# A chunked linear-attention kernel with a maxout feed-forward: units of two sequences, transposed attention output, and both layers side by side

## The chip, the cores and the metric

The kernel runs on one core of one Trainium2 chip. The metric is device time in microseconds (us), the median over repeated executions. A ratio below is the mean time of a kernel's fast runs over the mean time of the kernel before in the same rounds on the same chip, so it is not quite the ratio of the quoted medians. The engines are PE (matrix), DVE (vector), ACT (scalar, activation functions), POOL (general purpose) and SP, which only issues transfers here.

## The reference

```python
# attention: 4 sequences, 8 heads, 768 steps, head width 48
for t in range(S):
    cur = einsum('bhd,bhe->bhde', u[None] * k_t, v_t)
    y[:, :, t] = einsum('bhd,bhde->bhe', r_t, state + cur)
    state = w_t[:, :, :, None] * state + einsum('bhd,bhe->bhde', k_t, v_t)
# feed-forward on x = y as (3072 tokens, 384)
g = maximum(x @ w1, x @ w2)      # (384, 1024) each
out = g @ w_out                  # (1024, 384)
```

Both kernels use max(a, b) = (a + b + |a - b|)/2. The sum goes straight through a combined matrix wc = (w1 + w2) w_out, and only |x (w1 - w2)| has to be formed. The factor 1/2 is applied to the output in the kernel before, and to w_out once, at the start, in the changed one (the "scaling of w_out" below).

## The kernel before

A chunk is 128 steps of one sequence; there are 24. The decay products are the exponential of a running sum of ln w, which a matmul with a triangle makes. Each chunk loads its inputs, forms the decayed r and k, transposes them, builds a masked 128x128 product per head, multiplies it with v, adds the state's part, and updates the state. All attention comes first; the feed-forward follows from a buffer x_sb.

```python
            nc.scalar.activation(lw, wt, AF.Ln)                       # table load
            nc.tensor.matmul(excl_p, triU, lw...)                     # running sum
            nc.scalar.activation(Aexcl..., excl_p, AF.Exp)            # table load
            # ... (cut)
            for h in range(H):                                        # 16 a chunk
                nc.tensor.matmul(Wtot_p[:, h:h + 1], lw[:, h, :], ones_col)
            # ... (cut: transposes, masked product MTm)
            for h in range(H):
                nc.tensor.matmul(y_p[:, h * D:(h + 1) * D], MTm[:, h, :], vb[:, h, :],
                                 start=True, stop=(c == 0))           # 128 rows
                if c > 0:
                    nc.tensor.matmul(y_p[:, h * D:(h + 1) * D], rT[:, h, :],
                                     S_b[:, h, :], start=False, stop=True)   # 48 rows
            # ... (cut: y into x_sb, state update on DVE)
    # after all chunks:
        for fo in range(FO):
            g1 = mps.tile([C, MBN], F32, tag="g1")                    # one buffer
            # ... (cut: three matmuls into g1)
            nc.scalar.activation(gT[:, fo, :], g1, AF.Abs)
```

## Time and profile before

| | before |
|---|---|
| time | 424.39 us at first, 424.6 beside the changed kernel |
| head, attention, feed-forward | 46, 256, 120 us |
| PE, DVE, ACT busy in attention | 203, 189, 93 of 256 us |
| granted PE clock in attention | 0.51 |
| one chunk of one sequence, steady | 10.88 us |

The prediction below shows the windows, the timeline and the groups. Two more views matter. The first is the page's row of 40 equal slices of the span, in tenths; PEclk is the granted clock of PE.

```profile
PE   1158899887788887788887788875788778787872
DVE  1872667777877777777777877885122222232212
PEclk9998565555555555555555555555799999999997
```

Three quarters busy on both PE and DVE, at half the clock, and then a feed-forward with DVE mostly idle: after the seventh slice none has an engine at 90%. The second is one group (count, then busy us and mean ns, then idle time of the engine ahead of it and who ended it):

```profile
L210 PE MATMUL g<-xT,wd_sb 128*128 128x512 bf16 x138 | 41.4, 391 | 13.5 <-ACT gT L212 12.4
```

In the feed-forward PE waits 12.4 us for ACT, since g has one buffer.

### The profile page before, as it was taken

Reading aid. Unit: us, or ns where it says so; the run is one execution under the profiler, and the core shown is the slowest. Engines: PE = TensorE matmul, PEld = TensorE weight load, DVE = VectorE, ACT = ScalarE, POOL = GpSimd, SP = SyncE. Lnnn points to the kernel's source line nnn. Section 1 sums busy time; section 2 is a strip of 40 time slices with the busy share of each in tenths; the row PEclk is TensorE's granted clock in tenths of the full one; section 3 lists DMA queues with packets and bytes.
Section 4 is the critical chain, followed back from the end, with each engine's and each line's share of the span. In section 5 each row is a group of like instructions: output and inputs, shape, how many; then the busy total and the mean of one; then the engine's idle time right before and its main releaser. Section 6 shows DMA issues by size and latency. Waiting matters only on the chain.

```text
span 422.0 us, 5555 instructions
## 1 busy us (share of the span) xinstructions
PE 314.5 (75%) x2078; PEld 189.2 (45%) x2088; DVE 244.0 (58%) x596; ACT 142.7 (34%) x206; POOL 2.7 (1%) x16
## 2 busy tenths in 40 slices
PE   1158899887788887788887788875788778787872
PEld 0125666555455554555555455542333334343331
DVE  1872667777877777777777877885122222232212
ACT  1014652444444443443333532100233243323320
POOL 2000000000000000000000000000000000000000
PEclk9998565555555555555555555555799999999997
DMA  7995242442433333433344222000001111110111
GB/s 293 186 251 91 53 80 56 76 74 57 82 75 66 70 68 57 89 67 72 74 75 76 56 57 57 2 0 0 2 25 50 33 44 37 39 50 29 54 43 51
DMA packets 112076, 28.67 MB, mean 68 GB/s; under 512 B 101041, under 2 KB 111282, under 8 KB 112050
## 3 DMA queue, kind: packets, MB, share of 16 engines
q1 hardware_dynamic: 112050, 28.32, 32.5%
q8 instruction: 16, 0.26, 0.3%
q14 instruction: 10, 0.08, 0.1%
HBM read 23.59 MB, written 4.72 MB: 67 GB/s over the span
## 4 chain that ended last, share of the span: by engine, by line
PE 53%; DVE 18%; ACT 17%; DMA 6%; issue 5%; SPq 0%; ACTq 0%; DVEq 0%
PE g L210 9%; PE Wtot_p L141 7%; PE y_p L168 6%; ACT gT L212 6%; PE y_p L171 6%; PE op L216 5%; ACT L116 5%; PE tp_k L154 5%; DVE MTm L164 4%; PE mt_p L163 3%; DVE x_sb L175 3%; PE op L219 3%; PE tp_r L153 3%; DVE S_new L184 2%; DMA w2f<-in_moe_w_dram 2%
## 5 line engine op out<-in xcount | busy, mean ns | idle before, releaser
L118 PE MATMUL excl_p<-lw,triU 128*128 128x384 f32 x48 | 38.8, 910 | 34.2 <-DVE incl L122 33.5
L143 ACT ACTIVATE Wtot_b<-Wtot_p 48x384 f32<-48x384 f32 x24 | 11.6, 484 | 120.8 <-DVE S_new L184 119.6
L210 PE MATMUL g<-xT,wd_sb 128*128 128x512 bf16 x138 | 41.4, 391 | 13.5 <-ACT gT L212 12.4
L205 DVE COPY xT<-tp 128x128 bf16<-128x128 bf16 x72 | 16.1, 224 | 54.0 <-PE tp L204 54.0
L212 ACT ACTIVATE gT<-g 128x512 bf16<-128x512 f32 x48 | 28.7, 597 | 53.5 <-PE g L210 52.7
L216 PE MATMUL op<-gT,wo_sb 128*128 128x512 bf16 x140 | 41.6, 381 | 3.8 <-ACT gT L212 2.5
L227 DVE CAST osx<-tp 128x128 f32<-128x128 bf16 x72 | 20.8, 289 | 40.7 <-PE tp L225 27.6
L168 PE MATMUL y_p<-vb,MTm 128*128 128x48 bf16 x192 | 38.1, 220 | 5.7 <-DVE MTm L164 5.7
L141 PE MATMUL Wtot_p<-ones_col,lw 128*48 128x1 f32 x384 | 33.2, 216 | 5.2 <-ACT lw L116 3.5
L141 PEld LDWEIGHTS Wtot_p<-ones_col,lw 128*48 128x48 f32 x384 | 31.2, 186 | 10.5 <-ACT lw L116 7.8
L171 PE MATMUL y_p<-S_b_new,rT 48*128 48x48 bf16 x160 | 34.8, 218 | 0.0
L156 DVE COPY kT<-tp_k 48x512 bf16<-48x512 bf16 x48 | 19.9, 414 | 23.2 <-PE tp_k L154 23.1
L164 DVE TENSOR_TENSOR MTm<-mt_p,maskU 128x512 bf16<-128x512 f32 x48 | 31.0, 686 | 2.7 <-PE mt_p L163 0.2
L153 PE MATMUL tp_r<-ident,rp 128*48 128x128 bf16 x192 | 29.8, 308 | 2.8 <-DVE rp L127 2.5
L153 PEld LDWEIGHTS <-rp 128*48 128x48 bf16 x192 | 18.3, 145 | 26.9 <-DVE vb L131 16.2
L154 PE MATMUL tp_k<-ident,kp 128*48 128x128 bf16 x192 | 29.8, 309 | 0.7 <-DVE kT L156 0.4
L163 PE MATMUL mt_p<-rT,kT 48*128 48x128 bf16 x192 | 28.3, 302 | 0.5 <-DVE kT L156 0.5
L116 ACT ACT_TABLE_LOAD x22 | 28.2, 1283 | 1.1 <-PEq L248 0.7
L118 PEld LDWEIGHTS excl_p<-lw,triU 128*128 128x128 f32 x48 | 11.8, 305 | 37.0 <-DVE incl L122 35.8
L120 ACT ACT_TABLE_LOAD x22 | 28.2, 1283 | 0.4
L210 PEld LDWEIGHTS <-wd_sb 128*128 128x128 bf16 x144 | 13.9, 98 | 31.7 <-issue 22.8
L168 PEld LDWEIGHTS <-MTm 128*128 128x128 bf16 x192 | 18.4, 106 | 19.3 <-DVE MTm L164 12.5
(56 smaller groups left out, 408.2 us busy)
## 6 DMA issues: line engine op xcount, KB each, us to landing
rt<-in_r_dram SPq DMA_DIRECT2D x24, 192.0 KB, 3.8
kt<-in_k_dram SPq DMA_DIRECT2D x24, 192.0 KB, 3.6
vt<-in_v_dram SPq DMA_DIRECT2D x24, 192.0 KB, 2.7
wt<-in_w_dram SPq DMA_DIRECT2D x24, 192.0 KB, 3.1
out_dram<-osx SPq DMA_DIRECT2D x72, 64.0 KB, 1.5
w1f<-in_moe_w_dram SPq DMA_DIRECT2D x1, 1536.0 KB, 6.4
w2f<-in_moe_w_dram SPq DMA_DIRECT2D x1, 1536.0 KB, 9.9
wof<-in_moe_w_out_dram SPq DMA_DIRECT2D x1, 1536.0 KB, 7.1
```

The lines of the kernel that those rows point to most:

```text
L116: nc.scalar.activation(lw, wt, AF.Ln)
L118: nc.tensor.matmul(excl_p, triU, lw.rearrange("a b c -> a (b c)"))
L141: nc.tensor.matmul(Wtot_p[:, h:h + 1], lw[:, h, :], ones_col)
L153: nc.tensor.transpose(tp_r[:, j, :], rp[:, h, :], ident)
L154: nc.tensor.transpose(tp_k[:, j, :], kp[:, h, :], ident)
L163: nc.tensor.matmul(mt_p[:, j, :], kT[:, h, :], rT[:, h, :])
L164: nc.vector.tensor_mul(MTm[:, half * 4:half * 4 + 4, :], mt_p, maskU4)
L168: nc.tensor.matmul(y_p[:, h * D:(h + 1) * D], MTm[:, h, :], vb[:, h, :], start=True, stop=(c == 0))
L171: nc.tensor.matmul(y_p[:, h * D:(h + 1) * D], rT[:, h, :], S_b[:, h, :], start=False, stop=True)
L210: nc.tensor.matmul(g1, wd_sb[:, ko, fo * C:(fo + 1) * C], xT[:, ko, :], start=(ko == 0), stop=(ko == KO - 1))
L212: nc.scalar.activation(gT[:, fo, :], g1, AF.Abs)
L216: nc.tensor.matmul(op, wo_sb[:, fo, ko * C:(ko + 1) * C], gT[:, fo, :], start=(fo == 0), stop=False)
```

## The change

The intent is to let attention and feed-forward run on the engines at the same time, with fewer and longer instructions and a single load of ACT's tables. A unit is one chunk of two sequences (12 units). The output of attention is made already transposed, in slices of 128 columns, so the feed-forward needs no transposes. Because a head has 48 columns and a slice has 128, v and the state are kept in zero-padded rows (vz, S_z), and a matmul takes a 128-wide window of such a row. The feed-forward of unit i-1 is written after the attention of unit i. The diff, cut to its core:

```diff
+    units = [(c, bp) for c in range(NC) for bp in range(B // NB)]
+    nc.scalar.preload_act_table_set("natural_log_exp_and_others")
 # ... inputs: one tile of [C, 2 sequences, H, D] each instead of [C, H, D]
-            Wtot_p = psum.tile([D, H], F32, tag="wt")
-            for h in range(H):
-                nc.tensor.matmul(Wtot_p[:, h:h + 1], lw[:, h, :], ones_col)
+            row = dram.tile([1, NB * HD], F32)      # last row of incl out to DRAM
+            nc.sync.dma_start(out=row, in_=incl[C - 1:C]...)
+            for ab in range(2):                     # and back, transposed
+                nc.sync.dma_start(out=Wt[ab * DP:ab * DP + D]..., in_=row...[ab])
+            nc.scalar.activation(Wx, Wt, AF.Exp)
-            vb = sbuf.tile([C, H, D], BF16, tag="vb")
-            nc.vector.tensor_copy(vb, vt)
+        nc.gpsimd.tensor_copy(vz[...], t["v"])      # POOL
 # ... transposes: two heads (padded to 64 rows each) in one
-                nc.tensor.matmul(y_p[:, h * D:(h + 1) * D], MTm[:, h, :], vb[:, h, :], ...)
-                if c > 0:
-                    nc.tensor.matmul(y_p[:, h * D:(h + 1) * D], rT[:, h, :], S_b[:, h, :], ...)
+            for j in range(KO):
+                nc.tensor.matmul(y_p[:, j, :], vd[:, b, j * C:(j + 1) * C], ident, ...)
+            if c > 0:
+                for p, j, o in s_win:
+                    nc.tensor.matmul(y_p[:, j, :], S_z[bp][:, b, p * SS + o:p * SS + o + C],
+                                     rkT[:, 0, p, :], ...)
+            for n, (h, j, o) in enumerate(v_win):
+                nc.tensor.matmul(y_p[:, j, :], vz[:, b, h * VS + o:h * VS + o + C],
+                                 MTm[:, h % 2, h // 2, :], ...)
+            nc.scalar.copy(xT[:, :, b, :], y_p)
 # ... state update on DVE, its bf16 copies on POOL
+    t = load(0); load_w12(); t_next = load(1); load_wo()
+    for i in range(len(units)):
+        xT = attention(i, t)
+        if i == 0:
+            prep_weights()
+        if prev is not None:
+            feed_forward(i - 1, prev)       # g in two buffers, output not transposed
+        prev = xT
+        # ... load(i + 2)
```

## The prediction

Passages on the hardware that no trace of the kernel before showed are cut from the text below, and each cut is marked. One cut is a term of the forecast's sum: an allowance for DVE held up by POOL, which took the walk's period from 14.0 to 14.8 us. The sum still has it: 42 + 10 x 14.8 + 15 + 2.4 = 207.4 us.

> **What bounds the kernel now.** I read four views: the windows table, the timeline of one steady chunk, the groups, and the chain of waits in the last stage. The windows first (busy us and count of each engine, then granted clock, DMA share, GB/s):
>
> ```profile
> 0.00:46.00 46.00, 20.39 (x140) 12.98 (x140) 23.70 (x37) 12.17 (x17) 2.66 (x16) 0.92 0.93 193
> 46.00:302.00 256.00, 203.20 (x1489) 134.86 (x1490) 188.73 (x431) 92.81 (x127) 0.00 (x0) 0.51 0.31 59
> 302.00:422.00 120.00, 90.92 (x450) 41.34 (x458) 31.56 (x128) 37.67 (x64) 0.00 (x0) 0.98 0.14 40
> ```
>
> There are three stages one after the other: a head of 46 us that waits for transfers, an attention stage of 256 us, and a feed-forward of 120 us. In attention PE is 79% busy but at a granted clock of 0.51; in the feed-forward it runs at 0.98, and DVE is idle for three quarters of it. Neither stage uses what the other leaves free.
>
> The timeline shows a chunk repeating every 10.9 us (the table load of L116 starts at 143.37 and 154.24). What fills PE in it is not arithmetic:
>
> ```profile
> 157.80 0.53 PE L180 MATMUL kv_p<-vb,kp 128*48 128x48 bf16 x8
> ...
> 160.51 0.22 PE L168 MATMUL y_p<-vb,MTm 128*128 128x48 bf16 x1 [0.21 <-DVE MTm L164]
> 160.66 0.22 PE L171 MATMUL y_p<-S_b_new,rT 48*128 48x48 bf16 x1
> 160.81 0.22 PE L168 MATMUL y_p<-vb,MTm 128*128 128x48 bf16 x1
> ```
>
> Eight alike kv_p matmuls of 48 columns take 0.53 us, so (0.53 - 0.22)/7 = 0.045 us each. The y_p matmuls of the same 48 columns, which alternate between 128 and 48 rows of the array, start 0.15 us apart: 0.1 us is lost at each change of form, 16 times a chunk.
>
> ```profile
> L118 PE MATMUL excl_p<-lw,triU 128*128 128x384 f32 x48 | 38.8, 910 | 34.2 <-DVE incl L122 33.5
> L141 PE MATMUL Wtot_p<-ones_col,lw 128*48 128x1 f32 x384 | 33.2, 216 | 5.2 <-ACT lw L116 3.5
> L164 DVE TENSOR_TENSOR MTm<-mt_p,maskU 128x512 bf16<-128x512 f32 x48 | 31.0, 686 | 2.7 <-PE mt_p L163 0.2
> L116 ACT ACT_TABLE_LOAD x22 | 28.2, 1283 | 1.1 <-PEq L248 0.7
> L120 ACT ACT_TABLE_LOAD x22 | 28.2, 1283 | 0.4
> ```
>
> The 44 table loads cost ACT 56 us, and in every chunk one of them and the Wtot_p matmuls behind it are on the chain. In the feed-forward the chain is a handshake, because one buffer holds g:
>
> ```profile
> 303.60 0.82 PE g L210 x3
> 304.44 0.61 ACT gT L212
> 305.09 0.82 PE g L210 x3
> 305.93 0.61 ACT gT L212
> ```
>
> Each fo costs 1.49 us of which PE streams 0.65.
>
> [...]
>
> **The change part by part.** A unit is one chunk of two sequences, and there are 12. I count each engine's work per unit at durations of this trace.
>
> DVE. In a run of instructions the starts are closer than the durations: three of 384 elements start at 153.86, 154.33 and 154.80, so 0.47 us each; the 3072-element subtraction takes 3.36 against 0.545 us, so 1.05 ns an element and 0.07 us fixed. That gives 0.87 us for 768 and 1.14 us for 1024 elements. Per unit: incl 2 x 0.47; rp, kp, ku twice, the reduce and vd 6 x 0.87 = 5.2; the masked product 2 x 1.14; the state 3 x 0.47; the rkT copies 2 x 0.62 (the 128x1024 bf16 copy from PSUM took 0.69 with its fixed part). The sum is 11.1 us, against about 8 a chunk, or 16 for two, before. Gone are the casts of v and S, the add into x_sb, both transposing copies of the feed-forward, and half of the fixed costs.
>
> PE at full clock. A 512-column matmul streams in 0.215 us (three take 0.81, one 0.38), 0.42 ns a column. The feed-forward is 24 x 256 + 22 x 384 columns = 6.1 us. Attention has 16 transposes, 16 mt_p and 38 y_p matmuls of 128 columns, at an estimated 0.065 us (half of the 0.105 measured at half clock, plus something; two 128-column ones started 0.06 apart in the feed-forward): 4.5 us. ex_p in fp32 2 x 0.7, kv_p 0.5, six changes of form 0.6. The sum is 13.2 us; the arithmetic grows (padded windows), but the 384 Wtot_p matmuls and the alternation go. At half clock it would be about 25 us.
>
> ACT: Ln and Ainv 0.8 each, Aex 2 x 0.42, four gT 2.1, xT and osb 1.7, Wx 0.2: 6.4 us, no table loads. POOL: the v copy and two state copies, perhaps 2 us. Input transfers: four loads of 192 KB were issued one a microsecond while the queue was full (12.10 to 16.3), so 8.4 us a unit: hidden, if the period exceeds it.
>
> Clock. Matmuls other than transposes stream about 9 us of a 14 us unit. In the feed-forward before, it is 12 of 20 us, at clock 0.98. So I take full clock.
>
> Order. I walked one unit through the orders in which the engines' instructions are built. From MTm of sequence 1: PE does the rest of o_p and the y windows, then ex_p of the next unit at about 4.3 us, and DVE waits some 0.9 us for it; Aex, incl, rp; kp waits about 0.7 us for Ainv, which stands behind a gT on ACT; g_p is paced by ACT until about 8; then the k transposes, rkT at 9.4, MTm of sequence 0 at 11, mt_p of sequence 1 done at 13.9. So the period is about 14.0, set by turns by PE and DVE.[...]
>
> Head. Unit 0 loads first (1.57 MB, 8.3 us), then w1 and w2 (3.1 MB, about 9.5 us as before), unit 1 (8.3 us), w_out (about 5 us): w_out lands near 34 us, where it landed at 25.4. DVE's scaling of w_out stands ahead of unit 1's rkT, and the 24 wc_p matmuls (5.5 us[...]) stand ahead of its mt_p. So MTm of unit 1 starts at about 42 us. Ten periods later unit 11 is there; its rest (3 us), y, g_p, o_p of the last feed-forward and its store take about 15 us. Time = 42 + 10 x 14.8 + 15 + 2.4 (time less span before) = 207.4; I say 208.
>
> **The rivals.**
> - The clock stays low:[...] attention before ran at 0.50 while 79% busy. Then PE binds at 25 us: 42 + 250 + 18 = 310 us. Against it: the feed-forward matmuls lie throughout the unit[...]. 5%; a partly low clock (period 18, 240 us) another 10%.
> - A new wait: the row of incl goes to DRAM and comes back through the same queue as the loads in 4-byte pieces, and Wx waits for it on ACT ahead of xT. I place its landing near 11.5 us after the unit's start and its use at 14. If each of the transfers takes 2 us longer, it stands on the path: period 17, 230 us.
> [...]
> - Everything overlaps better than in my walk and PE alone binds: period 13.2, 191 us.
> - The gain of the overlap fails and only fixed costs are saved: attention 200 and feed-forward 90, about 340. Nothing in the order supports it.
>
> **Range and chances.** One microsecond of the period is 10 us of the time. A period of 13 to 17.5 with the same head and tail gives 189 to 234; I take 188 to 240. Even the worst rival named stays 20% below 424, so faster is nearly sure: 0.98, with 0.01 each for the rest.
>
> **What would show it right or wrong.** Right: no ACT_TABLE_LOAD but the first; clock above 0.9 from 60 us on; a spacing of 14 to 15.5 us between the ex_p pairs; DVE near 75% and PE near 85% busy in the steady part; the first MTm of unit 1 at 40 to 44 us; waits of DVE for ex_p and Ainv of under 1 us a unit. Wrong: a clock near 0.5 (first rival); ACT's longest wait being Wx for its transfer (second);[...] a steady period outside 13 to 17.5; or a head beyond 50 us.

## The result, and the profile after

The changed kernel took 192.44 us (192.05 to 193.31, four runs) beside 424.6 us (424.07 to 424.91, four runs); the ratio is 0.4537, with a 95% interval of 0.4525 to 0.4549. The profiled run took 193.31 us at a mean clock of 0.998.

The slices of the kernel after (rows as before) show one busy stage behind a head:

```profile
PE   0615875389999989999999999999999999999992
DVE  0169998975747988999899799798997997937300
PEclk9999999999999999999999999999999999999999
```

Two windows, the end of the head and one steady unit (busy us and count of PE, weight loads, DVE, ACT and POOL, then granted clock, DMA share, GB/s):

```profile
30.00:40.00 10.00, 5.30 (x38) 2.80 (x38) 9.29 (x12) 2.07 (x3) 0.00 (x0) 1.00 1.00 189
...
108.65:121.30 12.65, 12.36 (x138) 8.69 (x137) 11.34 (x16) 6.67 (x13) 2.43 (x3) 1.00 0.77 154
```

One unit takes 12.65 us in the steady part. It holds two chunks of attention and the feed-forward of 256 tokens. PE is busy for 12.36 us of it and DVE for 11.34. Before, two chunks took 21.8 us and the feed-forward of 256 tokens a further 10 us (120/12).

The handshake is nearly gone (groups view): PE's idle time ahead of g fell from 13.5 to 1.1 us.

```profile
L262 PE MATMUL g_p<-xT,wd_sb 128*128 128x256 bf16 x288 | 39.8, 272 | 1.1
```

The timeline of one steady unit shows what is packed how densely:

```profile
105.88 1.30 PE L272 MATMUL o_p<-wo_sb,gT 128*128 128x384 bf16 x7
107.02 0.81 PE L158 MATMUL ex_p<-lw,triU 128*128 128x384 f32 x2
...
108.39 0.56 DVE L160 TENSOR_TENSOR incl<-ex_p,lw 128x384 f32<-128x384 f32 x1 [0.95 <-ACT Aex L159]
...
112.59 0.40 PE L209 MATMUL mt_p<-rkT 48*128 48x128 bf16 x8
114.89 0.72 PE L225 MATMUL y_p<-MTm,vz 128*128 128x128 bf16 x10 [0.20 <-DVE MTm L210]
```

With about 0.22 us for a lone matmul (the median of L225 is 219 ns), ten y_p matmuls in 0.72 us are (0.72 - 0.22)/9 = 0.056 us apart. The eight mt_p matmuls, which read 48 rows from row 0 and 48 from row 64 by turns, are (0.40 - 0.22)/7 = 0.026 us apart. Busy time takes in the tail of each burst and pauses shorter than it, so it is not all work. At the measured spacings (0.109 us for g_p, 0.163 for o_p, 0.325 for ex_p, 0.0125 for kv_p) the matmuls of a unit add up to 11.1 us of its 12.65. PE and DVE (11.34) thus have about the same amount of work, and neither alone fills the unit. DVE's only long wait is 0.95 us: its ex_p stands in PE's order behind seven o_p matmuls, and Aex (0.49 us on ACT) comes before incl.

The head is the rest of the story. Its timeline, just before unit 1 gets going:

```profile
37.17 1.75 DVE L111 TENSOR_SCALAR wo_sb<-wof 128x3072 bf16<-128x3072 f32 x1
...
38.98 6.57 PE L120 MATMUL wc_p<-wo_sb,wsT_sb 128*128 128x384 bf16 x24 [1.48 <-DVE wo_sb L111]
45.48 0.40 PE L209 MATMUL mt_p<-rkT 48*128 48x128 bf16 x8
...
45.92 1.23 DVE L210 TENSOR_TENSOR MTm<-mt_p,triU 128x1024 bf16<-128x1024 f32 x1 [2.11 <-PE mt_p L209]
```

The 24 wc_p matmuls take 6.57 us, but not evenly: the first 16 start 0.32 us apart, the last eight 0.163, as the same 384 columns do in the steady part (seven in 1.30, less 0.33 for one, over six: 0.162). So PE ran at half rate until about 44 us, though the record of its clock shows full speed there (1.00 from 30 to 40 and from 40 to 60 us); read PEclk and the mean clock of this profile with that in mind. The first masked product of a unit (MTm) starts at 45.92 for unit 1, 63.50 for unit 2, and 175.60 for unit 11. So the profiled time is 45.9 (head) + 129.7 (ten units) + 15.9 (tail) + 1.8 (time less span).

### The profile page after: what moved, and what is told of

It is laid out like the page before. It is cut to its first block, busy times and chain, and to the rows that moved or that the text cites. A ratio compares the mean times of both kernels' runs of the same rounds, so it can differ in the third digit from the quotient of the medians.

```text
span 191.5 us, 3963 instructions
## 1 busy us (share of the span) xinstructions
PE 163.8 (86%) x1624; PEld 111.7 (58%) x1624; DVE 145.3 (76%) x184; ACT 83.3 (43%) x158; POOL 41.3 (22%) x52
## 4 chain that ended last, share of the span: by engine, by line
PE 48%; DVE 25%; issue 8%; ACT 8%; DMA 5%; SPq 3%; POOL 1%; ACTq 0%; DVEq 0%; POOLq 0%
PE o_p L272 13%; PE g_p L262 8%; PE y_p L225 7%; DVE MTm L210 6%; PE ex_p L158 5%; DVE sf L241 5%; DVE ku L186 4%; PE o_p L269 4%; ACT gT L265 4%; PE wc_p L120 3%; DMA u_b<-in_u_dram 3%; ACT Ainv L163 3%; SPq L130 3%; PE y_p L217 3%; PE mt_p L209 3%
## 5 line engine op out<-in xcount | busy, mean ns | idle before, releaser
L262 PE MATMUL g_p<-xT,wd_sb 128*128 128x256 bf16 x288 | 39.8, 272 | 1.1
L272 PE MATMUL o_p<-wo_sb,gT 128*128 128x384 bf16 x192 | 40.0, 327 | 0.0
L265 ACT ACTIVATE gT<-g_p 128x512 bf16<-128x512 f32 x48 | 27.9, 596 | 12.0 <-PE g_p L262 11.7
L210 DVE TENSOR_TENSOR MTm<-mt_p,triU 128x1024 bf16<-128x1024 f32 x24 | 29.3, 1221 | 3.5 <-PE mt_p L209 3.2
L158 PE MATMUL ex_p<-lw,triU 128*128 128x384 f32 x48 | 23.1, 567 | 7.9 <-ACT lw L153 6.7
L160 DVE TENSOR_TENSOR incl<-ex_p,lw 128x384 f32<-128x384 f32 x24 | 13.3, 554 | 21.3 <-ACT Aex L159 21.3
L272 PEld LDWEIGHTS <-gT 128*128 128x128 bf16 x192 | 17.8, 98 | 10.0
L166 POOL CAST vz<-vt 128x768 bf16<-128x768 f32 x12 | 11.1, 928 | 47.0 <-DMA vt<-in_v_dram 38.2
L225 PEld LDWEIGHTS <-vz 128*128 128x128 bf16 x240 | 16.2, 102 | 6.5 <-issue 4.5
L225 PE MATMUL y_p<-MTm,vz 128*128 128x128 bf16 x240 | 18.4, 226 | 1.7 <-DVE MTm L210 1.7
L269 PE MATMUL o_p<-wc_sb,xT 128*128 128x384 bf16 x72 | 17.3, 326 | 0.0
L203 DVE COPY rkT<-tp 128x1024 bf16<-128x1024 bf16 x24 | 16.4, 683 | 0.5 <-PE tp L200 0.5
```

The lines of the kernel that those rows point to most:

```text
L158: nc.tensor.matmul(ex_p, triU, lw[:, b].rearrange("p h d -> p (h d)"))
L160: nc.vector.tensor_add(incl[:, b].rearrange("p h d -> p (h d)"), ex_p, lw[:, b].rearrange("p h d -> p (h d)"))
L203: nc.vector.tensor_copy(rkT, tp)
L210: nc.vector.tensor_mul(MTm.rearrange("p a q c -> p (a q) c"), mt_p.rearrange("p a q c -> p (a q) c"), triU.unsqueeze(1).to_broadcast([C, H ...
L225: nc.tensor.matmul(y_p[:, j, :], vz[:, b, h * VS + o:h * VS + o + C], MTm[:, h % 2, h // 2, :], start=False, stop=(n == len(v_win) - 1), s ...
L262: nc.tensor.matmul(g_p[:, q, :], wd_sb[:, ko, fo * C:(fo + 1) * C], xT[:, ko].rearrange("p b c -> p (b c)"), start=(ko == 0), stop=(ko == ...
```

## The experiments

Twelve kernels ran. The kernel before gave medians of 424.52, 425.42 and 424.83 us in them, so times of different calls can be compared to about 0.3%. First come the parts of the gain, then what bounds the kernel after, then the head.

### Fixed costs of the kernel before, one at a time and together

**The tables loaded once.**

```diff
+    nc.scalar.preload_act_table_set("natural_log_exp_and_others")
```

> The kernel before, with the one added line that loads the table set with both exp and ln once. Theory (table loads are on the chain of each chunk): one load of 1.18 us per chunk leaves the chain, so 24 x 1.2 = 28 us off, about 396 us; at most both loads, 56 us, 368 us. Rival (ACT has slack, it is 36% busy in this stage): within 2% of 424 us.

Measured: 416.4 us (two runs), ratio 0.9806 (0.9739 to 0.9874). The interval rules out that nothing changed, but leaves room for a gain under 2%. All loads but the first are gone and ACT's busy time falls from 142.7 to 85.2 us (1.34 us for each of the 43 loads), yet the steady chunk only falls from 10.88 to 10.46 us. The groups view shows a wait that did not change (the line numbers are one higher than before):

```profile
L119 PE MATMUL excl_p<-lw,triU 128*128 128x384 f32 x48 | 38.8, 910 | 34.2 <-DVE incl L123 33.4
```

PE's wait for DVE ahead of the running sum is as long as before, 34.2 us. The chain of waits tells more. In a chunk of the kernel before (142 to 154 us) it does run through a load, 1.18 us of it, and the logarithm behind it to Wtot_p. Here it runs from the state update through incl on DVE (0.48 us) and the running sum on PE (1.65 us) to Wtot_p. So the prediction read the chain rightly, but a second one was only 0.42 us a chunk shorter: 57 us of ACT work were worth 8 us. The theory's 396 us missed; the rival (within 2%) held.

**The y matmuls in two groups.** All eight products with 128 rows come first, then all eight with 48 rows.

```diff
             for h in range(H):
                 nc.tensor.matmul(y_p[...], MTm[:, h, :], vb[:, h, :],
-                                 start=True, stop=(c == 0))
-                if c > 0:
+                                 start=(h == 0), stop=(c == 0 and h == H - 1))
+            if c > 0:
+                for h in range(H):
                     nc.tensor.matmul(y_p[...], rT[:, h, :],
-                                     S_b[:, h, :], start=False, stop=True)
+                                     S_b[:, h, :], start=False, stop=(h == H - 1))
```

> The kernel before, with the y matmuls in two groups of eight (all 128-row ones, then all 48-row ones) instead of alternating. Theory (each change of form costs 0.1 us and y stands on the chain): 16 matmuls at 0.15 us become 16 at 0.045 us plus one change, 1.6 us a chunk less, so about 424 - 24 x 1.5 = 388 us. Rival (the 0.15 us is the cost of any accumulating matmul with new weights): spacing stays 0.15 us and the time 424 us.

Measured: 401.46 us, ratio 0.9454 (0.9384 to 0.9525). The timeline of a chunk:

```profile
150.75 0.50 PE L173 MATMUL y_p<-S_b_new,rT 48*128 48x48 bf16 x8
```

Eight matmuls now take 0.50 us, 0.04 apart instead of 0.15, so the cost of alternating was real. (Before, a step onto the same columns and a step onto the next head's were both 0.15 us, so it is not the second write to the same columns. The edit also turns eight accumulation groups into one; that was not varied alone.) The theory's 388 us missed: of 36 us, 23 came. A chunk takes 9.73 us, 1.15 less than before. In the attention window (46 to 278 us) PE falls from 203 to 174 busy us while DVE keeps its 187, so DVE now leads.

**Both together.** The two edits above in one kernel.

> The kernel before with both of its fixed costs repaired: the tables loaded once, and the y matmuls in two groups of eight. Theory (each repair alone ran into DVE and the half clock: 416.4 and 401.5 us): together they save about the sum or a little more, 8 + 23 = 31 us, 388 to 395 us, with DVE above 85% busy in the attention stage. Rival (each repair was hidden behind the other): 360 to 375 us.

Measured: 391.3 us (two runs), ratio 0.921 (0.9177 to 0.9242). A chunk takes 9.30 us: 1.58 less than before, against 0.42 + 1.15 of the two alone. The costs simply add up.

```profile
46.00:268.00 222.00, 166.71 (x1482) 115.66 (x1481) 187.04 (x430) 39.53 (x86) 0.00 (x0) 0.52 0.34 67
```

DVE is busy for 84% of this window, and the clock is still 0.52 while PE is 75% busy. Repairing the old structure would have given 33 of the 232 us.

### The changed kernel without one of its parts

**Attention first, feed-forward after it.** All twelve outputs are kept, and the feed-forward runs in a loop of its own at the end.

```diff
-        xT = mlp.tile([C, KO, NB, C], BF16, tag="xT", bufs=3)
+        xT = x_all[:, i]
 ...
-        if prev is not None:
-            feed_forward(i - 1, prev)
+        xTs.append(xT)
 ...
+    for i in range(len(units)):
+        feed_forward(i, xTs[i])
```

> The changed kernel with all feed-forwards after all attentions (pools released in between as in the kernel before). Theory (the rewritten attention alone is bound by the VectorE at 11.4 us a unit plus waits, and the feed-forward alone by TensorE at 6.1 to 7 us): attention about 13 us a unit, feed-forward 12 x 6.7 = 80 us, total 46 + 11 x 13 + 80 = 265 to 275 us, so the overlap is worth 75 to 80 us. Rival (the feed-forward beside it is what keeps the clock up): granted clock near 0.5 in attention, TensorE work of attention 6.5 us a unit at full clock becomes 13 and then binds, period 15 to 17 us, total 290 to 315 us.

Measured: 256.47 us (two runs), ratio 0.604 (0.5993 to 0.6087), less than the theory's 265 to 275. Windows of its two stages:

```profile
60.00:160.00 100.00, 67.72 (x716) 48.26 (x715) 92.36 (x122) 29.68 (x58) 14.69 (x24) 0.78 0.61 113
...
172.00:253.00 81.00, 78.23 (x542) 52.36 (x539) 0.00 (x0) 39.73 (x72) 0.00 (x0) 1.00 0.16 59
```

Attention alone takes 11.86 us a unit and is bound by DVE (92%). The clock falls to a mixed 0.78, but PE has slack there (68% busy). The feed-forward alone takes 81 us and is bound by PE (97%), with DVE idle. Putting the second beside the first costs 12.97 - 11.86 = 1.1 us a unit and saves most of the 81 us: the overlap is worth 256.5 - 192.4 = 64 us, where 75 to 80 were expected.

This gives a ladder of the 232 us: 33 us from the two fixed costs, 135 us from the rest of the rewrite (391.3 to 256.5: attention from 18.6 to 11.9 us for two chunks, feed-forward from 120 to 81 us), and 64 us from the overlap. The middle step is the largest, and no run takes it apart. The windows say this much: DVE leads attention in both kernels, and its busy time in that stage falls from 187 to 113 us (of 222 and 126 us); in the feed-forward PE's share rises from 77% to 97%.

**Without the preload.**

```diff
-    nc.scalar.preload_act_table_set("natural_log_exp_and_others")
```

> The changed kernel without the preload line: two table loads a unit return on ACT (2.6 us, ACT 6.7 to 9.3 of 12.65 us). Theory (ACT has slack now): at most 0.5 us a unit, 192 to 198 us. Rival (Wx, behind a load, delays xT and the ex_p evacuation that the VectorE waits for): 1.2 us or more a unit, 206 us or more.

Measured: 203.15 us in the three fast runs (202.29 to 203.31; a fourth, slow, took 205.33), ratio 0.4779 (0.4751 to 0.4806), between the theory and the rival. The 24 loads of 1.28 us cost 10.7 us here, at least as much as 44 of them cost before (8.1 us, 5.3 to 11.1 by its interval). The query of Wx in this kernel's trace (that profile was slow, so I use it only to see which wait exists) shows where they stand:

```profile
  ACT Wx L179: 20.9, 10
```

DVE waits ten times for the state's decay, whose exponential stands behind a load in ACT's order. No wait for Wx stands in the steady part of the kernel after. My reading is that the denser kernel has less to hide a load behind.

### What bounds the kernel after

Four kernels add or remove work on one engine.

**More PE work:** every transpose of r and k is done twice (16 x 0.056 us x 12 units = 10.8 us).

```diff
-                    nc.tensor.transpose(tp[:, q, p, :], src[...], ident)
+                    for _ in range(2):
+                        nc.tensor.transpose(tp[:, q, p, :], src[...], ident)
```

> The changed kernel with every transpose of r and k done twice (same result): 16 more of 0.056 us, 0.9 us of TensorE work a unit. Theory (TensorE binds the steady unit: 12.36 of 12.65 us busy): period 13.5 us, 11 x 0.9 = 10 us more, 202 us. Rival (the VectorE's in-order queue binds and TensorE has room): under 3 us more, 195 us. The scheduler builds another order for it, so the trace has to be read with the time.

Measured: 205.85 us (204.0 to 205.93), 13.4 more; the theory said 10.

```profile
60.00:180.00 120.00, 116.44 (x1321) 82.53 (x1319) 98.65 (x128) 55.10 (x109) 20.00 (x25) 1.00 0.66 136
```

PE stays 97% busy, and DVE falls to 82%. The units take 12 to 15.5 us by turns, so the order moved too, which is my guess for the 2.6 us beyond the added work.

**More DVE work:** the reduction is done twice (12 x 0.87 = 10.4 us).

```diff
         nc.vector.reduce_sum(dg, ku..., axis=AX.X)
+        nc.vector.reduce_sum(dg, ku..., axis=AX.X)
```

> The changed kernel with the reduction of ku done twice (same result): 0.87 us of VectorE work a unit, 11.35 to 12.2 of 12.65. Theory (TensorE binds; VectorE waits 1.25 us a unit and can take it in): 192 to 195 us. Rival (a loop through both engines binds): 11 x 0.87 = 9.6 us more, 202 us. The scheduler builds another order for it too.

Measured: 197.92 us (197.68 to 198.96), 5.5 more: neither the theory (192 to 195) nor the rival (202). PE is 93% busy and DVE 96% (107.3 and 110.3 of the 115 us from 60 on). About half of the addition is absorbed: DVE stands close behind PE.

**More POOL work:** each POOL copy is done twice, which adds 20 us of POOL time from 60 to 172 us.

```diff
         nc.gpsimd.tensor_copy(vz[...], t["v"])
+        nc.gpsimd.tensor_copy(vz[...], t["v"])
 # ... and the copies of the state likewise
```

> The changed kernel with each copy on GpSimd done twice (v and state; same result, same order on the other engines): its work goes from 2.4 to about 4.8 us a unit. Theory (where the two meet, GpSimd is the one that waits; its state copies take 0.5 to 1.1 us while the VectorE's durations stay at 0.95): VectorE durations unchanged, time 192 to 194 us. Rival of the prediction (VectorE is held up by GpSimd):[...] 200 us or more.

Measured: 193.02 us (192.35 to 193.87), 0.6 more, and the steady unit stays at 12.65 us. DVE's busy time from 60 to 172 us goes from 99.5 to 100.1. The queries of rp and ku, two DVE products of 768 elements a row, and of POOL's copy of the state, in the kernel after (min/median/max ns):

```profile
L164 DVE TENSOR_TENSOR rp<-rt,Aex x12: 947/949/951, 10.8 to 171.6; 128x768 bf16<-128x768 f32 x12
L185 DVE TENSOR_TENSOR ku<-kt,u_b x12: 947/954/1260, 12.5 to 157.1; 128x768 f32<-128x768 f32 x12
L248 POOL CAST sz<-sf x20: 500/802/1121, 43.1 to 158.5; 48x384 bf16<-48x384 f32 x20
```

In each steady unit ku starts 0.22 us before the first state copy, and the copy is the longer one: it takes 1.10 us, where the second copy, with no DVE product beside it, takes 0.50. In two early units it is the other way round: a copy had begun first, and ku took 1.06 us (at 69 us) and 1.26 us (at 82 us) instead of 0.95. So the two do lengthen each other's instructions here, and in these cases it was the one that began second that took longer. In the steady order that is POOL, which has time to spare (busy 21.3 of the 112 us), so the prediction's allowance of 0.8 us a unit for DVE came to nothing. (With the copies doubled, rp and kp too take longer in early units, up to 1.28 and 1.21 us.)

**Less PE work:** only half of the w_out matmuls of each output (the result is wrong).

```diff
-            for fo in range(FO):
+            for fo in range(FO // 2):
```

> The kernel after with only half of the w_out matmuls of each output (8 of 16 a unit, 0.163 us each, so 1.3 us of PE a unit taken away; the result is wrong on purpose). Theory (PE sets the period, DVE with 11.35 us a unit stands just behind it): the period falls from 12.65 to 11.6 to 12.0 us, DVE is then 95% busy in the steady part, and the time is 182 to 186 us. Rival (the period is set by the waits of the order between engines, not by PE): the period stays above 12.4 and the time above 190 us. If PE alone set it, the period would be 11.35 and the time 178 us.

Measured: 186.76 us (186.61 to 186.88), 5.7 less, though 96 x 0.163 = 15.6 us of PE work are gone. The mean unit from 2 to 11 falls from 12.46 to 12.05 us.

```profile
60.00:172.00 112.00, 102.67 (x1161) 71.96 (x1161) 103.89 (x133) 58.98 (x115) 19.81 (x25) 1.00 0.73 147
```

DVE (93%) has taken PE's place (92%), and both still lose some time to each other. The theory had the direction and the new bound, and gave 182 to 186 us: a little too much gain. No single bound holds: PE sets the period of the kernel after, but taking 1.3 us of PE work from a unit meets DVE after 0.4 us.

**Another order:** the DVE-heavy half of the next unit's attention is written ahead of the feed-forward, to take the 0.95 us wait away. The function is split in two:

```diff
-        xT = attention(i, t)
+        xT = attention_b(i, *nxt)
         # ... (weights, at i == 0)
+        if i + 1 < len(units):
+            nxt = attention_a(i + 1, t_next)
         if prev is not None:
             feed_forward(i - 1, prev)
```

> The changed kernel with the first half of the next unit's attention (Ln to vd) written ahead of the feed-forward, so that its ex_p comes ahead of the o_p matmuls. Theory (the VectorE's 0.95 us wait for Aex stands behind seven o_p matmuls; without it TensorE alone binds at 12.3 us): 12.65 to 12.3 us, 188 us. Rival (TensorE is already full, only the order changes): 191 to 194 us.

Measured: 194.52 us (194.09 to 195.0), 2.1 more, where the theory had 188 and the rival 191 to 194; the unit takes 12.86 us. The waits of DVE from 60 to 172 us (us in total, times, longest):

```profile
DVE rkT L208 <- PE tp L205: 9.0, 8, 1.4
DVE incl L160 <- ACT Aex L159: 0.7, 1, 0.7
```

The wait for Aex, 9.2 us in this window of the kernel after, is gone but for 0.7, and a wait of 9.0 us for PE's transposes has taken its place. PE was busy for 108.7 of these 112 us, against 109.0 in the kernel after: a wait of DVE is no loss while PE has no free time to give. Why the unit became longer, and did not just stay as it was, no run here shows.

### The head

**Weights earlier, less of their preparation on DVE.** The load of w_out goes ahead of unit 1's inputs, and four instructions go from DVE to ACT.

```diff
-        nc.vector.tensor_scalar_mul(wo_sb, wof, 0.5)
+        nc.scalar.mul(wo_sb, wof, 0.5)
 ...
-            nc.vector.tensor_copy(wsT_sb[...], tp)
+            nc.scalar.copy(wsT_sb[...], tp)
 ...
-    t_next = load(1)
     load_wo()
+    t_next = load(1)
```

> The kernel after, with the head rearranged: the load of w_out is issued ahead of unit 1's inputs, and the scaling of w_out (1.75 us) and the three copies of the transposed sum (0.69 us each) go from DVE to ACT. Theory (the head up to 45.9 us is set by DVE, which is busy 90% from 10 to 40 us, and by the late landing of w_out with 6.6 us of combined-weight matmuls behind it): the masked product of unit 1 starts at 38 to 41 us, the steady period stays 12.65, the time falls to 185 to 188 us. Rival (the transfers bound the head, the DMA engines are full for 40 us and unit 1's inputs land later by what w_out takes): it starts at 44 to 47 us and the time stays 191 to 194 us.

Measured: 192.02 us (191.34 to 193.85), ratio 0.4526 (0.4501 to 0.4551): the same as the kernel after. The timeline:

```profile
34.85 2.88 PE L120 MATMUL wc_p<-wo_sb,wsT_sb 128*128 128x384 bf16 x16
...
35.62 0.56 DVE L160 TENSOR_TENSOR incl<-ex_p,lw 128x384 f32<-128x384 f32 x1 [4.62 <-ACT Aex L159]
```

The combined weights are done at 37.7 instead of 45.5 us. But DVE now waits 4.62 us for unit 1's Aex, and unit 1's masked product starts at 44.24, only 1.7 us sooner. The numbers are the rival's, its reason is not shown: no wait for unit 1's transfers appears there. ACT starts unit 1's logarithm at 30.77 us, behind the moved work without a gap (the scaling takes 2.77 us there against 1.75 on DVE), where the kernel after started it at 23.62; and the running sum then stands on PE behind eight wc_p matmuls. Unit 2's starts at 57.37, 6.1 us sooner than in the kernel after, and that lead is lost again: units 2 to 11 take 13.2 us each instead of 12.46. The start of a unit was a poor measure of progress. PE's busy time summed up to 60 us is 40.4 us against 38.9, a lead of 1.5 us, and it is lost to PE's idle time later (106.1 busy of the 112 us from 60 on, against 109.0).

**Attention of unit 1 ahead of the weights.** The loads come in the order unit 0, unit 1, w1 and w2, w_out; the weights are prepared after unit 1; the moves to ACT are kept.

```diff
-    load_w12()
     t_next = load(1)
+    load_w12()
     load_wo()
 ...
-        if i == 0:
+        if i == 1:
             prep_weights()
```

> The kernel after, with the loads in the order unit 0, unit 1, w1 and w2, w_out, the weights prepared after the attention of unit 1 instead of unit 0, and the same two moves from DVE to ACT. Theory (PE idles 27 us of the head while DVE works; attention of unit 1 needs no weights and can fill it): the masked product of unit 1 starts at 28 to 32 us, the weights are ready at about 45 us with two units of attention done, and the time falls to 182 to 187 us. Rival (w_out lands at the same time, and the weights' chain of transposes and combined-weight matmuls now starts only when w1 and w2 have landed, at 33 us, so the feed-forward of unit 0 starts after 48 us): 189 to 196 us.

Measured: 193.06 us (192.24 to 193.2), ratio 0.454 (0.4527 to 0.4553): the same again. Its timeline:

```profile
29.12 1.22 DVE L210 TENSOR_TENSOR MTm<-mt_p,triU 128x1024 bf16<-128x1024 f32 x1
...
54.70 0.56 DVE L244 TENSOR_TENSOR sf<-sf,Wx 128x384 f32<-128x384 f32 x1 [9.06 <-ACT Wx L180]
```

Unit 1's masked product starts at 29.12, 17 us sooner. But the combined weights are finished at 47.5 us, 2 us later than in the kernel after. The first feed-forward starts only then, Wx stands in ACT's order behind its outputs, and DVE waits 9.06 us. The rival was right. In all three kernels PE is idle for about 20 us of the first 40 (21.0, 18.5 and 19.4 us) and nearly full from there on. The feed-forward's weights come through transfers that keep the DMA engines full for those 40 us (a share of 0.96 to 1.13 in each ten of them, in all three kernels), and that is my reading of why PE cannot be given more to do. Two rivals stand untested: DVE, busy for 23.7 to 28.6 of these 40 us, with the weights' preparation in its order, and the half rate of PE, at which at least 16, 8 and 14 of the 24 wc_p matmuls ran in the three kernels (0.32 us apart). Neither order made the head cheaper, and whether smaller transfers would, no run here shows.

## Why the prediction was right or wrong

**Right: the direction, the mechanism, the range.** 192.4 us lies within 188 to 240. The full clock, taken over from the feed-forward before (0.98), held: 1.00 from 60 us on. That it follows from the share of matmuls, as the prediction argued, was not shown. One table load is left. The work per unit was well sized on three engines: DVE 11.1 predicted and 11.34 measured, ACT 6.4 and 6.7, POOL 2 and 2.4. The tail was 15 and took 15.9. Of the prediction's own signs these came true: one load, the clock, and DVE's waits under 1 us each. Missed were the spacing of 14 to 15.5 us, DVE near 75% and PE near 85% busy (90% and 98% in the steady unit), and the first MTm of unit 1 at 40 to 44 us; and one sign of being wrong appeared, a steady period outside 13 to 17.5 us.

**In part luck: the sum.** Ten periods took 129.7 us, 18.3 less than the 148 foretold; the head, the tail and the time less span together came out 4.2 us longer than foretold (45.9, 15.9 and 1.8 against 42, 15 and 2.4). The two misses offset each other in part, so 207.4 is nearer to the time than its period deserved.

**Mis-sized: the steady period, 14.8 against 12.65 us** (12.97 in the mean of ten units). Three terms of it failed.

- PE's work was put at 13.2 us, a sum of spacings; the spacings measured 11.1 (12.36 is busy time, with tails and short pauses). The term for 128-column matmuls was 0.065 us; it measured 0.056, and 0.026 for the 16 that read 48 rows each. That is 54 x 0.009 + 16 x 0.039 = 1.1 us of the 2.1. Most of the rest is the 0.6 us for changes of form, which the spacings leave out, and kv_p and ex_p, at 1.5 us instead of 1.9.
- The walk put DVE's wait for ex_p and for Ainv on the path and came to 14.0 us. The waits exist as foretold (0.95 and 0.30 us; the walk had 0.9 and 0.7), but the early-order run shows that removing the first gains nothing. The walk also placed all 24 g_p matmuls ahead of the k transposes, as in an early unit; in most steady units 19 stand there, and the other five are 0.5 us (0.109 each).
- The allowance for POOL (14.0 to 14.8 us), an estimate that rested on no trace, had the wrong side waiting: in the steady order POOL's copy takes longer (1.10 us against 0.50) and DVE's product does not (0.95), and the doubled copies cost 0.6 us in the whole run.

**Mis-sized: the head, 42 against 45.9 us.** The chain was right: scaling of w_out, then wc_p, then unit 1. The step that failed is the landing of w_out at 34 us as what starts it: DVE ran the scaling at 37.17 with no wait before it, because it was over 90% busy from 20 to 40 us (9.8 and 9.3 us of each ten). The wc_p matmuls took 6.57 instead of 5.5 us, since 16 of them ran at half rate (0.32 us apart against 0.163). The two head kernels did not win this miss back by reordering.

**Wrong about the kernel before: which costs stood on the chain.** "In every chunk one of them ... on the chain" overrated the table loads. One did stand on the chain, but the next chain was only 0.42 us shorter, and so much were the 2.6 us of loads worth in a steady chunk. The alternation of y matmuls (16 changes at 0.1 us) was worth 1.15 us a chunk. Neither entered the predicted time, which was built from the work after, so this error did not reach the sum.

**The rivals.** The nearest was "PE alone binds", 191 us. It holds for the order of the engines but not by itself: less PE work finds DVE next in line after a third of the gain. That its 191 us lies so near is partly luck: its period of 13.2 us was a PE sum that was 2 us too large, with no waits. The low clock did not come; with the same attention and no feed-forward beside it, in the serial kernel, it was 0.78. The wait for Wx exists in the head (0.96 and 2.79 us) and not in the steady units.

## What to carry to other kernels

Look for two stages that starve different engines (here DVE-bound attention and PE-bound feed-forward) and run them side by side: here a unit of both took 12.97 us, where the longer of the two took 11.86 alone, and the granted clock was 1.00 (PE 97% busy) against 0.78 in the attention alone (68%). Busy time alone did not tell the clock: PE was 79% busy at 0.51 (attention before), 76% at 0.98 (feed-forward before) and 75% at 0.52 (attention with both repairs). Judge progress by the busy time of the engine that binds, not by when some instruction starts: a reorder that started units 6 us sooner gained nothing. Before repairing a visible wait, ask whether the engine it waits for has time left to give; a wait of 9 us was removed here and came back as another of 9 us.
